# A gated recurrence followed by a gated unit: from per-batch units of six windows to a planned stream of flattened 512-token blocks

**Chip and metric.** One core of one Trainium2 chip runs the whole program. The time is device microseconds (us). A run is several executions, of which the median is quoted; single executions of the changed kernel spread by about 1.4%, those of the kernel before by 0.6%. The program does not leave its one core. The engines are called PE (matrix multiply; PEld is its weight load), DVE (VectorE, elementwise work and scans), ACT (ScalarE, tanh, exp and square root), POOL (GpSimd) and SP (issues transfers). SBUF is the on-chip memory, and PSUM is the memory that takes PE's products.

## The reference, cut to what matters

```python
# B, S, D = 4, 6336, 256; float32 in and out
a_t     = exp(8 * sigmoid(r_gate) * log(clip(sigmoid(a_param))))     # per token and channel
x_gated = sqrt(max(1 - a_t*a_t, 1e-6)) * sigmoid(i_gate) * x
for t in range(S):                                                   # recurrence over time
    h = a_t[:, t] * h + x_gated[:, t]
    y[:, t] = h
gate = sigmoid(causal 5-tap convolution of y over time, per channel)
val  = y @ w_val
out  = (gate * val) @ w_out
```

The recurrence is the only thing that orders the tokens, and it starts anew at each of the four batches. The kernel writes every sigmoid as 0.5 + 0.5 tanh, so that ACT's tanh and exp follow each other without loading another activation table. The square root does not: in the trace of the kernel before, a table load stands in front of each of the 12 square-root instructions and another behind each.

## The kernel before

Channels lie on the 128 partitions (two halves, h) and time on the free axis. A batch of 6336 tokens is cut into twelve windows of 512 and one of 192; six windows make a unit (6, 6 and 1 for each batch). A unit runs tanh and exp for all its windows, then one square root over the whole unit, then the scans. The output half (`backend`) of a window runs two windows later.

```python
unit_list = [win_list[i0:i0 + 6] for i0 in range(0, len(win_list), 6)]
...
for b in range(B):
    for unit in unit_list:
        for (wt0, wnt) in unit:
            # loads in the order x, r, i
            ...
            nc.scalar.activation(out=tri[:], in_=ri[:], func=ACT.Tanh, scale=0.5)
            nc.vector.scalar_tensor_tensor(out=u2[:], in0=ti, scalar=1.0, in1=xt[:], ...)   # "u"
            ...                                        # PE transposes, ACT exp -> ach
            nc.gpsimd.tensor_tensor(out=e_pl[...], in0=ach[...], in1=ach[...], op=ALU.mult) # squares
        nc.scalar.activation(out=n_pl[:, :, 0:utok], in_=e_pl[:, :, 0:utok], func=ACT.Sqrt, ...)
        for wi, (wt0, wnt) in enumerate(unit):
            ...                                        # PE transposes u -> uT
            nc.vector.tensor_tensor(out=xg[...], in0=uT[...], in1=n_pl[...], op=ALU.mult)
            nc.gpsimd.tensor_copy(out=yb[:, :, 0:4], in_=prev_y[:, :, prev_nt:prev_nt + 4])
            for h in range(H):
                nc.vector.tensor_tensor_scan(out=yb[:, h, 4:4 + wnt], data0=ach[:, h, 0:wnt],
                                             data1=xg[:, h, 0:wnt], initial=yb[:, h, 3:4], ...)
            if len(pending) >= 2:
                flush_one()                            # backend of an earlier window
            pending.append((b, wt0, wnt, yb))

def backend(...):
    ...                                                # PE conv -> gp, ACT tanh -> tg, PE -> val
    nc.vector.scalar_tensor_tensor(out=gv[...], in0=tg[...], scalar=1.0, in1=val[...], ...)
    for each pair of 128-token tiles:                  # two in a full window
        ...                                            # PE: ops = gv @ wo
        nc.vector.tensor_scalar(out=osb[:, ii:ii + 2, :], in0=ops[:], scalar1=0.5, ...)
```

The order of the instructions on each engine is left to the framework's scheduler. All output copies are on VectorE.

Of the kernel before, what the change touches and what calls it, by code (L numbers as in the profile page):

```python
# [8 lines left out]
P = 128  # L10
WIN = 512
SUB = WIN // P
UNIT_WIN = 6
CONV_K = 5
C_SCALE = 8.0
FP32 = mybir.dt.float32
BF16 = mybir.dt.bfloat16
ACT = mybir.ActivationFunctionType
ALU = mybir.AluOpType


@with_exitstack
def kernel(
# [14 lines left out]
    H = D // P  # L38

    const = ctx.enter_context(tc.tile_pool(name="const", bufs=1))  # L40

    ident_f = const.tile([P, P], FP32, name="ident_f")
    make_identity(nc, ident_f[:])
    ident_b = const.tile([P, P], BF16, name="ident_b")
    nc.vector.tensor_copy(out=ident_b[:], in_=ident_f[:])

    with tc.tile_pool(name="ps_setup", bufs=2, space=bass.MemoryType.PSUM) as ps_setup:
        ap2 = const.tile([H, P], FP32, name="ap2")
        nc.sync.dma_start(ap2[:], a_param.rearrange("(h p) -> h p", p=P))
        kps = ps_setup.tile([P, H], FP32, name="kps")  # L50
        nc.tensor.transpose(out=kps[:], in_=ap2[0:H, :], identity=ident_f[0:H, 0:H])
        kt = const.tile([P, H], FP32, name="kt")
        nc.scalar.activation(out=kt[:], in_=kps[:], func=ACT.Tanh, scale=0.5)
        ksig = const.tile([P, H], FP32, name="ksig")
        nc.vector.tensor_scalar(out=ksig[:], in0=kt[:], scalar1=0.5, scalar2=0.5,
                                op0=ALU.mult, op1=ALU.add)
        nc.vector.tensor_scalar(out=ksig[:], in0=ksig[:], scalar1=1e-6, scalar2=1.0 - 1e-6,
                                op0=ALU.max, op1=ALU.min)
        kln = const.tile([P, H], FP32, name="kln")
        nc.scalar.activation(out=kln[:], in_=ksig[:], func=ACT.Ln)  # L60
        kf = const.tile([P, H], FP32, name="kf")
        nc.vector.tensor_scalar(out=kf[:], in0=kln[:], scalar1=C_SCALE, scalar2=None, op0=ALU.mult)
        khf = const.tile([P, H], FP32, name="khf")
        nc.vector.tensor_scalar(out=khf[:], in0=kln[:], scalar1=0.5 * C_SCALE, scalar2=None, op0=ALU.mult)

        wrow = const.tile([CONV_K, D], FP32, name="wrow")
        nc.sync.dma_start(wrow[:], moe_conv_w[:, :])
        wcol = []
        for h in range(H):
            wc_ps = ps_setup.tile([P, CONV_K], FP32, name="wc_ps")  # L70
            nc.tensor.transpose(out=wc_ps[:], in_=wrow[0:CONV_K, h * P:(h + 1) * P],
                                identity=ident_f[0:CONV_K, 0:CONV_K])
            wc = const.tile([P, CONV_K], FP32, name=f"wc{h}")
            nc.vector.tensor_copy(out=wc[:], in_=wc_ps[:])
            wcol.append(wc)
        diag = [[None] * CONV_K for _ in range(H)]
        for h in range(H):
            for kk in range(CONV_K):
                dg = const.tile([P, P], BF16, name=f"diag{h}_{kk}")
                nc.vector.tensor_scalar(out=dg[:], in0=ident_f[:], scalar1=wcol[h][:, kk:kk + 1],  # L80
                                        scalar2=None, op0=ALU.mult)
                diag[h][kk] = dg

    b025 = const.tile([P, 1], FP32, name="b025")
    nc.vector.memset(b025[:], 0.25)

    wv = const.tile([P, H, D], BF16, name="wv")
    nc.gpsimd.dma_start(wv[:], moe_w_val.rearrange("(hk p) n -> p hk n", p=P))
    wo = const.tile([P, H, D], BF16, name="wo")
    nc.gpsimd.dma_start(wo[:], moe_w_out.rearrange("(hk p) n -> p hk n", p=P))  # L90


    yring = ctx.enter_context(tc.tile_pool(name="yring", bufs=5))
    aring = ctx.enter_context(tc.tile_pool(name="aring", bufs=8))
    plane = ctx.enter_context(tc.tile_pool(name="plane", bufs=2))
    inp = ctx.enter_context(tc.tile_pool(name="inp", bufs=3))
    u2pool = ctx.enter_context(tc.tile_pool(name="u2pool", bufs=8))
    work = ctx.enter_context(tc.tile_pool(name="work", bufs=3))
    ps_cm = ctx.enter_context(tc.tile_pool(name="ps_cm", bufs=1, space=bass.MemoryType.PSUM))
    ps_conv = ctx.enter_context(tc.tile_pool(name="ps_conv", bufs=1, space=bass.MemoryType.PSUM))  # L100
    ps_val = ctx.enter_context(tc.tile_pool(name="ps_val", bufs=1, space=bass.MemoryType.PSUM))
    ps_out = ctx.enter_context(tc.tile_pool(name="ps_out", bufs=1, space=bass.MemoryType.PSUM))
    win_list = []
    t0 = 0
    while t0 < S:
        nt = min(WIN, S - t0)
        win_list.append((t0, nt))
        t0 += nt
    unit_list = []
    for i0 in range(0, len(win_list), UNIT_WIN):  # L110
        unit_list.append(win_list[i0:i0 + UNIT_WIN])
    max_unit_tok = UNIT_WIN * WIN

    def subtiles(nt):
        res = []
        p0 = 0
        j = 0
        while p0 < nt:
            npj = min(P, nt - p0)
            res.append((j, p0, npj))  # L120
            p0 += npj
            j += 1
        return res

    pending = []
    pstores = []

    def flush_store():
        if pstores:
            dst, srcap = pstores.pop(0)  # L130
            nc.sync.dma_start(dst, srcap)

    def backend(wb, wt0, wnt, yb):
        gp = ps_conv.tile([P, H, WIN], FP32, name="gp", tag="gp")
        for h in range(H):
            for kk in range(CONV_K):
                nc.tensor.matmul(  # L137
                    out=gp[:, h, 0:wnt],
                    lhsT=diag[h][kk][:],
                    rhs=yb[:, h, kk: kk + wnt],  # L140
                    start=(kk == 0), stop=(kk == CONV_K - 1),
                )
        tg = work.tile([P, H, WIN], BF16, name="tg", tag="tg")
        nc.scalar.activation(out=tg[:, :, 0:wnt], in_=gp[:, :, 0:wnt], func=ACT.Tanh, scale=0.5)  # L144
        val = ps_val.tile([P, H, WIN], FP32, name="val", tag="val")
        for m in range(H):
            for hk in range(H):
                nc.tensor.matmul(  # L148
                    out=val[:, m, 0:wnt],
                    lhsT=wv[:, hk, m * P:(m + 1) * P],  # L150
                    rhs=yb[:, hk, 4:4 + wnt],
                    start=(hk == 0), stop=(hk == H - 1),
                )
        gv = work.tile([P, H, WIN], BF16, name="gv", tag="gv")
        nc.vector.scalar_tensor_tensor(  # L155
            out=gv[:, :, 0:wnt], in0=tg[:, :, 0:wnt], scalar=1.0, in1=val[:, :, 0:wnt],
            op0=ALU.add, op1=ALU.mult,
        )
        sts = subtiles(wnt)
        osb = work.tile([P, SUB, D], FP32, name="osb", tag="osb", bufs=4)  # L160
        ii = 0
        full_window = (wnt == WIN)
        while ii < len(sts):
            pair = sts[ii:ii + 2]
            full_pair = len(pair) == 2 and pair[0][2] == P and pair[1][2] == P
            if full_pair:
                ops = ps_out.tile([P, 2, D], FP32, name="ops", tag="ops")
                for (js, p0, npj), slot in zip(pair, (0, 1)):
                    for hk in range(H):
                        nc.tensor.matmul(  # L170
                            out=ops[:, slot, :],
                            lhsT=gv[:, hk, p0:p0 + P],
                            rhs=wo[:, hk, :],
                            start=(hk == 0), stop=(hk == H - 1),
                        )
                nc.vector.tensor_scalar(out=osb[:, ii:ii + 2, :], in0=ops[:], scalar1=0.5, scalar2=None, op0=ALU.mult)  # L176
                if not full_window:
                    p0a = pair[0][1]
                    pstores.append((out[wb, wt0 + p0a:wt0 + p0a + 2 * P, :].rearrange("(j p) d -> p j d", p=P), osb[:, ii:ii + 2, :]))
                ii += 2  # L180
            else:
                (js, p0, npj) = pair[0]
                ops = ps_out.tile([P, 2, D], FP32, name="ops", tag="ops")
                for hk in range(H):
                    nc.tensor.matmul(
                        out=ops[0:npj, 0, :],
                        lhsT=gv[:, hk, p0:p0 + npj],
                        rhs=wo[:, hk, :],
# [138 lines left out]
```

## Time and profile before

| | kernel before |
|---|---|
| time, median of 3 executions (lowest to highest) | 441.89 us (441.31 to 443.02) |
| span of the profiled execution | 440.1 us |
| VectorE (DVE) busy, idle | 363.9, 76.2 us |
| ScalarE (ACT) busy | 291.5 us |
| DVE idle: first 60 us, 60 to 420, the rest | 33.3, 35.6, 7.3 us |

This is DVE's timeline of the kernel before (start, length, engine and line, operation, count, idle before):

```profile
45.70 0.69 DVE L273 TENSOR_TENSOR xg<-uT,n_pl 128x1024 bf16<-128x1024 bf16 x1 [5.50 <-ACT n_pl L257]
46.49 2.46 DVE L281 TENSOR_TENSOR_SCAN yb<-ach,yb,xg 128x512 bf16<-128x512 f32 x2
```

The gated input xg waits 5.5 us for the square root of all six windows, and only then, at 46.5 us, does the recurrence start.

### The profile page before, as it was taken

The page shows a single profiled execution, that of the slowest core. Times are in us where ns is not written, and L with a number is a line of the kernel's source. Part 1 is how long each engine was busy: PE and PEld are TensorE (multiplying, and loading weights), DVE is VectorE, ACT ScalarE, POOL GpSimd, SP SyncE. Part 2 cuts the span into 40 slices and gives each one's busy share as a digit, 9 for nine tenths or more (in the row PEclk, how much of TensorE's full clock was granted, in tenths as well). Part 3 has the DMA queues.
Part 4 walks back from the last instruction along what each step waited for, and adds up shares of the span by engine and source line. Part 5 has one row for each costly group of instructions (what it writes and reads, how often), then busy time and mean ns, then how long its engine had stood idle before and what let it go on. Part 6 is the DMA issues. An engine that isn't in the chain of part 4 may idle for free.

```text
span 440.1 us, 5342 instructions
## 1 busy us (share of the span) xinstructions
PE 293.1 (67%) x1931; PEld 168.7 (38%) x1931; DVE 363.9 (83%) x386; ACT 291.5 (66%) x253; POOL 120.3 (27%) x112
## 2 busy tenths in 40 slices
PE   0221777658884595969684689558876485758994
PEld 0221344334453253535343245233543243424442
DVE  2242899769997799879999899969997599978984
ACT  0988836792969847696958746897465984593111
POOL 2252202700535216402542202802063143300000
PEclk9999999889989598769999599988998689958998
DMA  8999958788769975896978887999886962211233
GB/s 236 348 348 348 316 182 252 257 257 254 238 214 314 331 222 177 273 337 209 295 234 251 275 277 241 283 297 316 251 266 206 335 207 95 73 70 49 95 125 133
DMA packets 105544, 104.43 MB, mean 237 GB/s; under 512 B 3623, under 2 KB 105518, under 8 KB 105518
## 3 DMA queue, kind: packets, MB, share of 16 engines
q1 hardware_dynamic: 104974, 103.83, 74.4%
q0 software_dynamic: 544, 0.26, 0.4%
q8 instruction: 15, 0.25, 0.2%
q14 instruction: 11, 0.09, 0.1%
HBM read 78.39 MB, written 25.95 MB: 237 GB/s over the span
## 4 chain that ended last, share of the span: by engine, by line
DVE 48%; ACT 20%; issue 13%; PE 11%; DMA 5%; POOL 2%; SPq 1%; DVEq 0%; POOLq 0%; ACTq 0%
DVE yb L281 24%; ACT n_pl L257 10%; DVE gv L155 8%; DVE osb L176 8%; DVE xg L273 6%; DMA ri<-in_i_gate_dram 5%; PE ops L170 3%; ACT tri L233 3%; ACT ach L252 3%; PE gp L137 3%; DVE u L234 2%; PE val L148 2%; POOL e_pl L255 2%; ACT L257 2%; PE srT L245 1%
## 5 line engine op out<-in xcount | busy, mean ns | idle before, releaser
L137 PE MATMUL gp<-yb,diag 128*128 128x512 bf16 (+1 forms) x520 | 139.2, 402 | 13.6 <-ACT tg L144 12.1
L281 DVE TENSOR_TENSOR_SCAN yb<-ach,yb,xg 128x512 bf16<-128x512 f32 (+1 forms) x104 | 144.9, 1431 | 1.2
L255 POOL TENSOR_TENSOR e_pl<-ach 128x1024 f32<-128x1024 f32 (+1 forms) x52 | 107.4, 2077 | 74.3 <-ACT ach L252 74.2
L144 ACT ACTIVATE tg<-gp 128x1024 bf16<-128x1024 f32 (+1 forms) x52 | 51.1, 983 | 88.4 <-PE gp L137 84.3
L170 PE MATMUL ops<-wo,gv 128*128 128x256 bf16 x384 | 62.9, 290 | 59.8 <-DVE gv L155 41.7
L233 ACT ACTIVATE tri<-ri 128x2048 bf16<-128x2048 f32 x48 | 90.4, 1910 | 1.9 <-DMA ri<-in_i_gate_dram 1.8
L252 ACT ACTIVATE ach<-srT,khf 128x512 f32<-128x512 bf16 (+1 forms) x104 | 71.9, 757 | 29.0 <-PE srT L245 28.8
L234 DVE SCALAR_TENSOR_TENSOR u<-tri,xt 128x1024 bf16<-128x1024 bf16 x48 | 69.0, 1437 | 25.2 <-ACT tri L233 25.2
L176 DVE TENSOR_SCALAR osb<-ops 128x512 f32<-128x512 f32 x96 | 65.0, 677 | 16.4 <-PE ops L170 16.1
L279 POOL COPY yb<-yb 128x8 bf16<-128x8 bf16 x48 | 10.8, 225 | 226.9 <-DVE yb L281 178.4
L137 PEld LDWEIGHTS <-diag 128*128 128x128 bf16 x520 | 50.4, 103 | 58.0 <-ACT tg L144 10.2
L170 PEld LDWEIGHTS <-gv 128*128 128x128 bf16 x384 | 36.3, 102 | 92.6 <-DVE gv L155 61.3
L267 PE MATMUL uT<-ident_b,u 128*128 128x128 bf16 (+1 forms) x400 | 40.5, 248 | 35.0 <-DVE xg L273 34.7
L155 DVE SCALAR_TENSOR_TENSOR gv<-tg,val 128x1024 bf16<-128x1024 bf16 (+1 forms) x52 | 60.0, 1154 | 3.1 <-ACT tg L144 3.1
L148 PE MATMUL val<-yb,wv 128*128 128x512 bf16 (+1 forms) x208 | 56.6, 388 | 0.0
L245 PE MATMUL srT<-ident_b,tri 128*128 128x128 bf16 (+1 forms) x400 | 36.2, 237 | 28.5 <-ACT tri L233 18.3
L273 DVE TENSOR_TENSOR xg<-uT,n_pl 128x1024 bf16<-128x1024 bf16 (+1 forms) x52 | 33.9, 653 | 23.1 <-ACT n_pl L257 22.7
L267 PEld LDWEIGHTS <-u 128*128 128x128 bf16 (+1 forms) x400 | 33.2, 112 | 50.5 <-issue 42.8
L257 ACT ACTIVATE n_pl<-e_pl,b 128x6144 bf16<-128x6144 f32 (+1 forms) x12 | 45.8, 3815 | 3.8 <-POOL e_pl L255 3.6
L245 PEld LDWEIGHTS <-tri 128*128 128x128 bf16 (+1 forms) x400 | 29.0, 106 | 39.6 <-ACT tri L233 20.3
L148 PEld LDWEIGHTS <-wv 128*128 128x128 bf16 x208 | 20.9, 102 | 16.8 <-issue 2.8
L257 ACT ACT_TABLE_LOAD x12 | 15.4, 1283 | 0.2
(32 smaller groups left out, 45.2 us busy)
## 6 DMA issues: line engine op xcount, KB each, us to landing
xt<-in_x_dram SPq DMA_DIRECT2D x48, 512.0 KB, 5.0
ri<-in_r_gate_dram SPq DMA_DIRECT2D x48, 512.0 KB, 5.8
ri<-in_i_gate_dram SPq DMA_DIRECT2D x48, 512.0 KB, 6.2
out_dram<-osb SPq DMA_DIRECT2D x48, 512.0 KB, 3.5
xt<-in_x_dram SPq DMA_DIRECT2D x4, 128.0 KB, 3.4
ri<-in_r_gate_dram SPq DMA_DIRECT2D x4, 128.0 KB, 3.3
ri<-in_i_gate_dram SPq DMA_DIRECT2D x4, 128.0 KB, 3.3
out_dram<-osb SPq DMA_DIRECT2D x4, 128.0 KB, 1.8
```

Source lines behind the costliest of these rows:

```text
L137: nc.tensor.matmul(out=gp[:, h, 0:wnt], lhsT=diag[h][kk][:], rhs=yb[:, h, kk: kk + wnt], start=(kk == 0), stop=(kk == CONV_K - 1),)
L148: nc.tensor.matmul(out=val[:, m, 0:wnt], lhsT=wv[:, hk, m * P:(m + 1) * P], rhs=yb[:, hk, 4:4 + wnt], start=(hk == 0), stop=(hk == H - 1),)
L155: nc.vector.scalar_tensor_tensor(out=gv[:, :, 0:wnt], in0=tg[:, :, 0:wnt], scalar=1.0, in1=val[:, :, 0:wnt], op0=ALU.add, op1=ALU.mult,)
L170: nc.tensor.matmul(out=ops[:, slot, :], lhsT=gv[:, hk, p0:p0 + P], rhs=wo[:, hk, :], start=(hk == 0), stop=(hk == H - 1),)
L176: nc.vector.tensor_scalar(out=osb[:, ii:ii + 2, :], in0=ops[:], scalar1=0.5, scalar2=None, op0=ALU.mult)
L233: nc.scalar.activation(out=tri[:], in_=ri[:], func=ACT.Tanh, scale=0.5)
L234: nc.vector.scalar_tensor_tensor(out=u2[:], in0=ti, scalar=1.0, in1=xt[:], op0=ALU.add, op1=ALU.mult)
L252: nc.scalar.activation(out=ach[:, h, 0:wnt], in_=srT[:, h, 0:wnt], func=ACT.Exp, scale=khf[:, h:h + 1], bias=khf[:, h:h + 1])
L255: nc.gpsimd.tensor_tensor(out=e_pl[:, :, wc0:wc0 + wnt], in0=ach[:, :, 0:wnt], in1=ach[:, :, 0:wnt], op=ALU.mult)
L257: nc.scalar.activation(out=n_pl[:, :, 0:utok], in_=e_pl[:, :, 0:utok], func=ACT.Sqrt, scale=-0.25, bias=b025[:, 0:1])
L267: nc.tensor.transpose(out=uT[:, h, p0:p0 + npj], in_=u2[0:npj, j, h * P:(h + 1) * P], identity=ident_b[0:npj, 0:npj],)
L281: nc.vector.tensor_tensor_scan(out=yb[:, h, 4:4 + wnt], data0=ach[:, h, 0:wnt], data1=xg[:, h, 0:wnt], initial=yb[:, h, 3:4], op0=ALU.mult ...
```

## The change

Its intent is to keep DVE and ACT both occupied by one stream that does not stop at batch ends. It has six parts.

1. The batches are flattened to 25344 tokens: 49 windows of 512 and one of 256. Windows that straddle a batch end are scanned in two segments, so the four short windows vanish.
2. Planes and pools become rings of eleven slots (a, e, u) and seven (y); the square root writes in place. The other pools change a little too: two product buffers for xg, gv and tg instead of three, three output buffers instead of four, and a scan takes its first value straight from the previous window and not from POOL's copy of it.
3. The square-root batches grow from one window (1, 3, 3, 4, 4, 5 and so on, as the plan finds work) instead of six at once.
4. The output copies go to DVE or ACT, whichever the plan says can start sooner (53 and 46), and the 0.5 moves into the weights.
5. The inputs are issued r, i, x, so that tanh can begin before x is there; three input buffers instead of four.
6. A list schedule built from a table of costs decides the order of all instructions, and the framework is told to keep it.

```diff
+NS = 11
+NY = 7
+NIN = 3
+MIN_UNIT = [1, 2, 3, 4]
+COST = dict(load=4.5, tanh=1.9, u2=1.3, ..., scan=2.7, ..., osbD=0.64, osbA=0.62, sq=0.88, table=1.3, ...)
+def make_plan(frac):
... each step: of all operations whose inputs are done, take the one that can start first
+            for e, eng in (("D", "DVE"), ("A", "ACT")):
+                cand("osb", eng, COST["osb" + e], [("out", q), ("store", qwin[q][0] - NOSB)], 0.5, q)
...
+            low = (nsq - at("scan")) * (COST["xg"] + COST["scan"]) <= 2 * COST["table"] + COST["sq"] * n
+            enough = n >= min(MIN_UNIT[min(len(units), len(MIN_UNIT) - 1)], nw - nsq)
+            if stuck or (low and enough):
+                cand("sq", "ACT", ...)
...
-    for b in range(B):
-        for unit in unit_list:
+    with tc.manual_schedule():
...
+        aring = rings.tile([P, NS, H, WIN], FP32, name="aring")
+        ering = rings.tile([P, NS, H, WIN], FP32, name="ering")
+        uring = rings.tile([P, NS, SUB, D], BF16, name="uring")
+        yring = rings.tile([P, NY, H, YW], BF16, name="yring")
...
-                        initial=yb[:, h, 3:4],
+                        initial=0.0 if fresh else py[:, h, pend - 1:pend],
...
-                nc.vector.tensor_scalar(out=osb[:, ii:ii + 2, :], in0=ops[:], scalar1=0.5, ...)
+            if eng == "DVE":
+                nc.vector.tensor_copy(out=dst, in_=ops[:])
+            else:
+                nc.scalar.copy(out=dst, in_=ops[:])
...
+        for (t, op, i, eng, n) in plan:
+            ops_by_name[op](i, eng, n)
```

## The prediction

> **What bounds the kernel now.** I read five views in this order: busy time by engine, busy time by stretch, the vector engine's waits, groups by shape, and the timeline around one square-root batch. All are of the kernel before.
>
> ```profile
> PE 293.1 (67%) x1931; PEld 168.7 (38%) x1931; DVE 363.9 (83%) x386; ACT 291.5 (66%) x253; POOL 120.3 (27%) x112
> HBM read 78.39 MB, written 25.95 MB: 237 GB/s over the span
> ```
>
> VectorE (DVE) is the fullest engine, yet it idles 440.1 - 363.9 = 76.2 us. The bytes are not the limit: a 1/40 slice of the early load-only phase moves 348 GB/s, and 104.4 MB at that rate are 300 us.
>
> ```profile
> 0.00:60.00 60.00, 19.85 (x124) 12.34 (x125) 26.68 (x38) 41.38 (x33) 16.05 (x19) 1.00 1.00 313
> 60.00:420.00 360.00, 260.20 (x1729) 149.03 (x1727) 324.44 (x331) 246.65 (x217) 104.02 (x92) 0.89 0.73 231
> 420.00:440.10 20.10, 13.08 (x82) 7.35 (x80) 12.80 (x19) 3.46 (x4) 0.19 (x1) 0.91 0.33 115
> ```
>
> Columns: stretch, length, busy us of PE, weight loads, DVE, ACT, POOL, then clock, DMA share, GB/s. DVE idles 33.3 us in the first 60, 35.6 (10%) in the middle and 7.3 at the end.
>
> ```profile
> DVE u L234 <- ACT tri L233: 25.2, 8, 7.9
> DVE xg L273 <- ACT n_pl L257: 22.7, 8, 5.5
> DVE osb L176 <- PE ops L170: 16.1, 22, 1.4
> ```
>
> The waits say why: for the first tanh results, for the square-root batch (one batch of six windows must be complete before any scan of it; the first scan starts at 46.5 us), and for the output product held in one PSUM buffer.
>
> ```profile
> L281 DVE TENSOR_TENSOR_SCAN yb<-ach,yb,xg 128x512 bf16<-128x512 f32 x96 | 135.2, 1446 | 1.1
> L234 DVE SCALAR_TENSOR_TENSOR u<-tri,xt 128x1024 bf16<-128x1024 bf16 x48 | 69.0, 1437 | 25.2 <-ACT tri L233 25.2
> L176 DVE TENSOR_SCALAR osb<-ops 128x512 f32<-128x512 f32 x96 | 65.0, 677 | 16.4 <-PE ops L170 16.1
> L155 DVE SCALAR_TENSOR_TENSOR gv<-tg,val 128x1024 bf16<-128x1024 bf16 x48 | 57.8, 1205 | 3.1 <-ACT tg L144 3.1
> L273 DVE TENSOR_TENSOR xg<-uT,n_pl 128x1024 bf16<-128x1024 bf16 x48 | 32.5, 678 | 23.1 <-ACT n_pl L257 22.7 <-PE uT L267 0.4
> ...
> L257 ACT ACT_TABLE_LOAD x12 | 15.4, 1283 | 0.2
> ```
>
> **What the Trainium skill says, and whether the trace agrees.** "ScalarE: Activation LUTs", section "What ACT_TABLE_LOAD costs": tables are loaded by set, exp and sqrt lie in different ones, and a switch is given as 1283 ns of load plus about 1380 of drain. The load agrees (1283); the drain does not appear:
>
> ```profile
> 86.63 5.42 ACT L257 ACTIVATE n_pl<-e_pl,b 128x6144 bf16<-128x6144 f32 x1 [0.75 <-POOL e_pl L255]
> 92.06 1.28 ACT L144 ACT_TABLE_LOAD   x1
> 93.35 1.02 ACT L144 ACTIVATE tg<-gp 128x1024 bf16<-128x1024 f32 x1
> ```
>
> The load starts 0.01 us after the square root ends and the tanh follows it at once, so I charge 1.28 us a switch. The same section gives an ACTIVATE with immediate operands as 186 ns + 0.833 ns an element: about 0.61 us for a 512-wide output copy on ACT (an estimate; no such copy runs before). "SBUF — State Buffer", section "Who interferes with whom": a DVE instruction with two SBUF inputs contends with a GpSimd instruction reading SBUF. The trace agrees: the scan's median is 1265 ns but its mean 1446, u's 1215 and 1437; both read two SBUF operands beside the squaring on POOL. The excess is 96 x 0.18 + 48 x 0.22 = 28 us. "VectorE: DVE Perf Modes", section "The perf-mode tier table": an fp32 operand in PSUM allows no faster mode. Hence folding 0.5 into the output weights makes the DVE copy no cheaper than today's 677 ns.
>
> **The change part by part.** The built order gives the counts: 49 windows of 512 tokens and one of 256 (49.5 in place of 48 full and 4 of 192), 53 output copies on DVE and 46 on ACT, 12 square-root units of 1, 3, 3, 4, 4, 5, 4, 4, 5, 5, 6 and a last 5.5 windows, in 23 instructions instead of 12.
>
> DVE work. One window without copies: (135.2 + 69.0 + 57.8 + 32.5) / 48 = 6.14 us; times 49.5 is 304. Copies: 53 x 0.677 = 36. Setup: 3. Sum 343 in row sums. The rows of before sum to 384 against 363.9 busy, since neighbours overlap, so I scale by 0.948: **325 us**, 39 less. Of that about 29 are the copies moved and about 10 are the short windows of 192, which cost nearly a full scan (1255 ns a half) for three eighths of the tokens.
>
> ACT work. tanh 49.5 x 1.91 = 95; exp 99 x 0.72 = 71; gate tanh 49.5 x 1.02 = 50; square root: a six-window call takes 5.42, so with the page's 0.28 us fixed part about 0.86 a window: 49.5 x 0.86 + 23 x 0.28 = 49; tables 27 x 1.28 = 35, as many as now; copies 46 x 0.61 = 28. Sum 328, and row sums against busy are 299 to 291.5 before: **319 us**, 28 more. So ACT and DVE come out almost equal. PE keeps its work (minus about 2% for padding) and POOL its 50 squarings; both have room.
>
> Start. Inputs are now issued r, i, x, so the first tanh needs 1 MB rather than 1.5 MB: about 8 us rather than 11.25. From there: tanh 1.9, transposes 1.0, exp 1.45, square 1.9, a second tanh in front of the load, table 1.28, square root 1.1, product 0.7: first scan near 18 us instead of 46.5. But unit two (windows 1 to 3) needs a table back, three tanh, three exp pairs, a gate tanh and a table, about 15 us of ACT, so its scans begin near 35. By then DVE has done about 15 us of work (setup 3, five u 6, one scan pair, product, gate, copies). After that it has as much work as ACT's next unit lasts (near 15 us each). **Start idle about 20 us, from 33.**
>
> End. The last unit leaves about eight windows of scans; the last window is half-sized. After its last scan come conv, gate, product, copy and store: about 8 us, of which DVE works 2 to 3. **End idle about 5 us.**
>
> DVE's path: 325 + 20 + 5 = 350. ACT's path: all but its last 9 gate tanh and 11 copies (319 - 16 = 303) must be done before the last scans can start, plus about 5 idle at the start, plus some 38 of DVE work and drain behind the last square root: 346. Two bounds within 1%.
>
> Middle. Two engines each at over 90%, fed in a fixed order, stall one another whenever a duration differs from the plan: a squaring that stretches a scan, a late load (three input buffers instead of four). DVE loses 10% there now; the batches come when the scans are about to run out instead of behind six windows, and the copies take the sooner engine, so I halve it: 5% of 340, **17 us**. This is the softest number. 350 + 17 = 367 of span, and 1.8 more for the measured time (441.9 against 440.1): **369 us**, 16% less.
>
> **The rivals.** First, ACT becomes the bound. For: 319 against 325, plus 12 batches whose table loads stop gate tanh and exp alike. Against: it waits 84 us for conv results today, waits that the interleaving can fill. If it also idles 8%, the time is near 380. Second, contention on the shared port grows: DVE leaves fewer gaps, so more of the 50 squarings fall beside a scan or u. If each costs 1 us rather than 28 / 48 = 0.6, that is 20 us more: 385 to 390. Third, loads become the bound: 104 MB in 365 us is 286 GB/s, 82% of the 348 seen, with three buffers. For: a store waiting in the in-order queue holds the loads behind it. Against: beyond the start, tanh waited 1.8 us for loads before, and a buffer has about three windows (20 us) to be refilled, while a load lands in 5 to 6 us. At worst 10 us. Fourth, the plan holds nearly perfectly and the middle loses 2%: 356.
>
> **Range and chances.** The rivals make 356 to 390; contention and ACT stalls together are possible but partly overlap in time. I take 355 to 386. To be within 2% it would have to lose 64 us of the 73 expected, more than any rival costs: faster 0.96, same 0.03, slower 0.01.
>
> **What would show it.** DVE busy 320 to 330 and ACT 315 to 325; first scan at 17 to 20 us; DVE idle near 20 us by 50 us; DVE waits for the square root well under 22.7 us beyond the start; table load still 1283 with no drain; DVE copies still near 677 ns and ACT copies near 610. A scan mean above 1500 ns means the contention rival; tanh waiting over 10 us for loads beyond the start means the load rival; ACT busier than DVE in the middle with DVE waiting for tanh or square root means the ACT rival. I am wrong if DVE busy does not fall by about 39 us, or if the middle loses over 10%.

## The result

| | before | after |
|---|---|---|
| time, median of 4 executions (lowest to highest) | 442.45 us (441.31 to 443.86) | 376.86 us (374.66 to 379.99) |
| span of the profiled execution | 440.1 us | 372.5 us |
| DVE busy, idle | 363.9, 76.2 us | 334.6, 37.9 us |
| ACT busy | 291.5 us | 312.4 us |

The ratio is 0.8516 (95% interval 0.8469 to 0.8563): 15% faster, and the outputs are correct. Ratios are the mean time of one kernel's fast executions over that of the other's in the same rounds, so not quite the ratio of the medians quoted here.

Busy time by engine (us, share of the span, instructions) and the bytes, after the change:

```profile
PE 272.4 (73%) x1933; PEld 159.9 (43%) x1933; DVE 334.6 (90%) x326; ACT 312.4 (84%) x298; POOL 138.3 (37%) x111
HBM read 78.39 MB, written 25.95 MB: 280 GB/s over the span
```

The span fell by 67.6 us. DVE's busy time gives 363.9 - 334.6 = 29.3 of it, DVE's idle time 76.2 - 37.9 = 38.3. So more than half of the gain is waiting that went, not work that moved.

Busy time by stretch after the change, with the columns that the prediction names:

```profile
0.00:60.00 60.00, 29.72 (x201) 17.75 (x202) 38.54 (x50) 51.40 (x46) 20.84 (x21) 0.89 1.00 313
60.00:360.00 300.00, 235.44 (x1686) 137.62 (x1685) 291.78 (x273) 257.03 (x248) 117.50 (x90) 0.95 0.86 279
360.00:372.50 12.50, 7.27 (x50) 4.50 (x47) 4.24 (x5) 3.96 (x6) 0.00 (x0) 0.93 0.41 147
```

DVE idles 21.5 us in the first 60, 300 - 291.78 = 8.2 us in the middle and 8.3 at the end. The middle, which lost 10% before, loses 2.7%.

DVE's waits after the change (us in total, times, longest):

```profile
DVE osb L367 <- PE ops L356: 8.0, 10, 1.7
DVE uring L246 <- ACT tri L240: 6.9, 6, 3.2
DVE xg L290 <- ACT ering L277: 6.2, 2, 5.0
```

These answer the three waits that the prediction shows, 16.1, 25.2 and 22.7 us before. The one for the square root happens twice in the whole program, both times at the start.

Groups by shape after the change (busy us, mean ns, then the idle time before and what ended it):

```profile
L306 DVE TENSOR_TENSOR_SCAN yring<-aring,yring,xg 128x512 bf16<-128x512 f32 x90 | 134.5, 1535 | 0.6
L246 DVE SCALAR_TENSOR_TENSOR uring<-tri,xt 128x1024 bf16<-128x1024 bf16 x49 | 66.8, 1369 | 7.0 <-ACT tri L240 6.9
L367 DVE COPY osb<-ops 128x512 f32<-128x512 f32 x53 | 36.1, 682 | 9.2 <-PE ops L356 8.0
...
L369 ACT COPY osb<-ops 128x512 f32<-128x512 f32 x46 | 27.2, 592 | 22.2 <-PE ops L356 19.1 <-issue 2.4 <-ACT tri L240 0.5
L277 ACT ACT_TABLE_LOAD x12 | 15.4, 1283 | 0.2
```

The copy costs DVE 682 ns, as the multiplying one cost 677, and ACT 592. The scan's mean rose from 1446 to 1535 ns, the only operation on DVE that became clearly dearer; u's mean fell from 1437 to 1369. The table load is as it was. On POOL the copy of the last four columns of a window became nearly three times as dear, before and after:

```profile
L279 POOL COPY yb<-yb 128x8 bf16<-128x8 bf16 x48 | 10.8, 225 | 226.9 <-DVE yb L281 178.4 <-PE srT L245 18.4 <-PE gp L137 11.9
L304 POOL COPY yring<-yring 128x8 bf16<-128x8 bf16 x49 | 31.6, 644 | 77.4 <-DVE yring L306 77.4
```

Little waits for it (PE's convolution, 1.3 us in all), and no run isolates why.

DVE's timeline around the first two square-root batches:

```profile
17.72 0.69 DVE L290 TENSOR_TENSOR xg<-uT,ering 128x1024 bf16<-128x1024 bf16 x1 [1.23 <-ACT ering L277]
18.45 2.34 DVE L306 TENSOR_TENSOR_SCAN yring<-aring,xg 128x512 bf16<-128x512 f32 x2
...
36.21 0.69 DVE L290 TENSOR_TENSOR xg<-uT,ering 128x1024 bf16<-128x1024 bf16 x1 [5.01 <-ACT ering L277]
36.94 2.46 DVE L306 TENSOR_TENSOR_SCAN yring<-aring,yring,xg 128x512 bf16<-128x512 f32 x2
```

The recurrence begins at 18.5 us instead of 46.5, does one window, and goes on at 36.9 when the next three windows have their square root.

### The profile page after: what moved, and what is told of

Read it like the earlier page. It is cut to its first block, busy times and chain, and to the rows that moved or that the text cites. A ratio compares the mean times of both kernels' runs of the same rounds, so it can differ in the third digit from the quotient of the medians.

```text
span 372.5 us, 5299 instructions
## 1 busy us (share of the span) xinstructions
PE 272.4 (73%) x1933; PEld 159.9 (43%) x1933; DVE 334.6 (90%) x326; ACT 312.4 (84%) x298; POOL 138.3 (37%) x111
## 4 chain that ended last, share of the span: by engine, by line
DVE 34%; ACT 23%; issue 19%; PE 14%; DMA 5%; POOL 2%; DVEq 0%; ACTq 0%
DVE yring L306 13%; DVE uring L246 8%; DVE gv L344 7%; ACT tri L240 6%; ACT ering L277 5%; PE gp L321 5%; PE ops L356 4%; ACT aring L257 4%; DMA xt<-in_x_dram 3%; DVE xg L290 3%; PE val L338 3%; ACT tg L327 3%; DVE osb L367 2%; ACT L327 2%; ACT L277 2%
## 5 line engine op out<-in xcount | busy, mean ns | idle before, releaser
L262 POOL TENSOR_TENSOR ering<-aring 128x1024 f32<-128x1024 f32 (+1 forms) x50 | 105.7, 2121 | 140.9 <-ACT aring L257 121.8
L321 PE MATMUL gp<-yring,diag 128*128 128x512 bf16 (+4 forms) x530 | 124.5, 384 | 24.7 <-DVE yring L306 14.2
L306 DVE TENSOR_TENSOR_SCAN yring<-aring,yring,xg 128x512 bf16<-128x512 f32 (+4 forms) x98 | 139.5, 1464 | 0.7
L240 ACT ACTIVATE tri<-ri 128x2048 bf16<-128x2048 f32 (+1 forms) x50 | 94.4, 1907 | 0.0
L321 PEld LDWEIGHTS <-diag 128*128 128x128 bf16 x530 | 50.8, 102 | 83.5 <-issue 16.3
L257 ACT ACTIVATE aring<-srT,khf 128x512 f32<-128x512 bf16 (+1 forms) x100 | 71.8, 791 | 3.4 <-PE srT L228 2.2
L246 DVE SCALAR_TENSOR_TENSOR uring<-tri,xt 128x1024 bf16<-128x1024 bf16 (+1 forms) x50 | 67.4, 1356 | 7.0 <-ACT tri L240 6.9
L344 DVE SCALAR_TENSOR_TENSOR gv<-tg,val 128x1024 bf16<-128x1024 bf16 (+1 forms) x50 | 59.7, 1194 | 2.5 <-PE val L338 1.7
L338 PE MATMUL val<-yring,wv 128*128 128x512 bf16 (+4 forms) x212 | 52.1, 371 | 5.3 <-DVE gv L344 5.3
L277 ACT ACTIVATE ering<-ering,b 128x3072 bf16<-128x3072 f32 (+2 forms) x21 | 47.0, 2280 | 0.1
L369 ACT COPY osb<-ops 128x512 f32<-128x512 f32 x46 | 27.2, 592 | 22.2 <-PE ops L356 19.1
L367 DVE COPY osb<-ops 128x512 f32<-128x512 f32 x53 | 36.1, 682 | 9.2 <-PE ops L356 8.0
L228 PE MATMUL uT<-ident_b,uring 128*128 128x128 bf16 x396 | 33.3, 232 | 15.0 <-DVE xg L290 14.7
L290 DVE TENSOR_TENSOR xg<-uT,ering 128x1024 bf16<-128x1024 bf16 (+1 forms) x50 | 33.7, 675 | 6.2 <-ACT ering L277 6.2
```

What stands on the lines that cost most here:

```text
L228: nc.tensor.transpose(out=dst[:, h, j * P:(j + 1) * P], in_=src[:, j, h * P:(h + 1) * P], identity=ident_b[:])
L240: nc.scalar.activation(out=tri[:, :, 0:nj, :], in_=ri[:, :, 0:nj, :], func=ACT.Tanh, scale=0.5)
L246: nc.vector.scalar_tensor_tensor(out=uring[:, g % NS, 0:nj, :], in0=tri[:, 1, 0:nj, :], scalar=1.0, in1=xt[:, 0:nj, :], op0=ALU.add, op1=A ...
L257: nc.scalar.activation(out=aring[:, g % NS, h, 0:ntok[g]], in_=srT[:, h, 0:ntok[g]], func=ACT.Exp, scale=khf[:, h:h + 1], bias=khf[:, h:h ...
L262: nc.gpsimd.tensor_tensor(out=ering[:, g % NS, :, 0:ntok[g]], in0=a, in1=a, op=ALU.mult)
L277: nc.scalar.activation(out=nring[:, sl:sl + k, 0:H * WIN], in_=ering[:, sl:sl + k].rearrange("p s h t -> p s (h t)"), func=ACT.Sqrt, scale ...
```

## Experiments

Twelve runs, in three calls, each with its own runs of the kernel before on the same chip. The changed kernel itself came to ratio 0.8516 beside its own runs of before and to 0.8463 in the last call, so ratios of different calls are compared with about 0.6% of doubt. Differences in us are taken from 376.86, the first call's figure, unless another is named; only the last call has its own run of the changed kernel. All medians are of four executions.

### The copies alone on DVE, same order

```diff
-            if eng == "DVE":
+            if True:
```

> The changed kernel in the same issue order, but all 99 output copies on DVE (46 moved back from ACT). Theory, DVE sets the pace (in the changed kernel it is busy 291.8 of the 300 us from 60 to 360): DVE busy rises by 46 x 0.61 = 28 us to about 362, ACT falls by 27 to about 285, and nearly all of it shows: about 403 us. Rival, ACT and DVE share the pace and ACT gains what DVE loses: half of it, about 390 us.

Measured: 407.13 us (405.91 to 408.83), ratio 0.9197 (0.9163 to 0.9232). Busy time by engine:

```profile
PE 284.3 (70%) x1933; PEld 162.2 (40%) x1933; DVE 362.6 (89%) x372; ACT 289.8 (71%) x252; POOL 133.4 (33%) x111
```

DVE is 362.6 - 334.6 = 28.0 us busier, and the time is 407.13 - 376.86 = 30.3 us longer. From 60 to 340 us DVE is busy 267.25 of 280 us (95%):

```profile
60.00:340.00 280.00, 206.00 (x1428) 118.31 (x1426) 267.25 (x260) 219.59 (x190) 107.47 (x79) 0.91 0.88 283
```

So with this order DVE sets the time, and what is put on it appears nearly in full: sharing the copies is worth 30 us here.

### The copies alone on ACT, same order

```diff
-            if eng == "DVE":
+            if False:
```

> The changed kernel in the same issue order, but all 99 output copies on ACT (53 moved from DVE at 0.59 us each). Theory, the split is near its balance: ACT busy rises by 31 us to about 343 and sets the pace, DVE falls to about 302: about 390 us, so the split beats both ends. Rival, DVE alone is short and ACT has room (43 idle us of the 300 in the middle): about 365 us.

Measured: 393.07 us (389.40 to 394.37), ratio 0.8873 (0.8817 to 0.8930). DVE is busy 302.6 us, ACT 337.7. From 60 to 340 us ACT has 259.8 of 280 us and DVE only 233.0; DVE waits for tanh 21.5 us, for the value product 18.7 and for the gate tanh 16.8:

```profile
60.00:340.00 280.00, 208.67 (x1476) 123.75 (x1499) 233.01 (x196) 259.80 (x272) 121.09 (x82) 0.92 0.89 287
DVE uring L246 <- ACT tri L240: 21.5, 16, 3.2
```

ACT is the fuller engine now, and the time is 16 us worse although DVE lost 32 us of work. The two runs together show that, in this order, neither engine alone should have the copies. The order was planned for the split; a plan made for all copies on one engine was not run.

### The framework's order in place of the planned one

```diff
-    with tc.manual_schedule():
+    if True:
```

The program is the same, copies, batches and rings too; only the order on the engines is left to the framework.

> The changed kernel with the same operations and buffers, but its order left to the framework's own scheduler instead of the list schedule's (correct result). Theory, the explicit order is what keeps the middle full: DVE idle between 60 and 360 us rises from 8 (2.7%) to about the 10% of the kernel before, +22 us, about 398 us. Rival, buffers, shared copies and small first batches carry the gain and any sensible order does: within 6 us, about 380 us.

Measured: 401.38 us (399.82 to 405.63), ratio 0.9080 (0.9019 to 0.9141). Its middle stretch, and its largest DVE wait:

```profile
60.00:360.00 300.00, 220.83 (x1554) 131.46 (x1555) 269.67 (x254) 258.23 (x244) 104.31 (x87) 0.89 0.84 271
```

```profile
DVE osb L367 <- PE ops L356: 25.2, 25, 3.0
```

DVE is busy 331.5 us in all, no more than with the planned order; but in the middle it idles 300 - 269.67 = 30.3 us instead of 8.2. So the order alone is worth 401.38 - 376.86 = 24.5 us, and it is won in idle time: 25 copies wait on DVE for an output product that PE has not finished, with everything behind them. The framework's order also changes tables more often, 33 loads instead of 27, and ACT is 8 us busier.

### Six windows in each square-root batch at least

```diff
-MIN_UNIT = [1, 2, 3, 4]
+MIN_UNIT = [6]
```

> The changed kernel planned with square-root batches of at least six windows from the first on (8 batches instead of 12). Theory, the growing batches are worth what they save at the start: first scan near 46 us instead of 18.4, DVE idle in the first 60 us near 35 instead of 21.5, middle unchanged, about 391 us. Rival, the eight table loads saved on ACT (4 batches, 10 us) and fuller batches give it back: within 4 us of the changed kernel, about 379 us.

Measured: 380.76 us (379.62 to 381.34), ratio 0.8592 (0.8561 to 0.8623); eight batches of 5 to 8 windows. First 60 us, and the first scan:

```profile
0.00:60.00 60.00, 20.86 (x153) 13.62 (x154) 27.14 (x39) 48.09 (x42) 22.31 (x20) 1.00 1.04 319
```

```profile
42.50 2.34 DVE L306 TENSOR_TENSOR_SCAN yring<-aring,xg 128x512 bf16<-128x512 f32 x2
```

The first scan is 24 us later, and DVE idles 54.2 us in all instead of 37.9. That is 16.3 us more, 11.4 of it in the first 60 us, where the theory held about 13.5. But the time is only 4 us longer, near the rival's number, because DVE is busy 325.1 us, 9.5 less. The plan answered the late start by giving six more copies to ACT (47 on DVE instead of 53; 6 x 0.68 = 4 us), and the scan's mean fell to 1467 ns. A late start was partly made good by moving work away from the engine that was late. Growing batches are worth some 4 us by this call and 6 against the last call's 374.94; the interval of the ratio just overlaps that of the first run of the changed kernel (0.8469 to 0.8563) and lies clear of the last one's (0.8426 to 0.8500). Either is far less than the 24 us by which the first scan comes earlier.

### No wide read of SBUF by POOL

```diff
-            nc.gpsimd.tensor_tensor(out=ering[:, g % NS, :, 0:ntok[g]], in0=a, in1=a, op=ALU.mult)
+            nc.gpsimd.memset(ering[:, g % NS, :, 0:ntok[g]], 0.25)
+            nc.gpsimd.tensor_tensor(out=ering[:, g % NS, :, 0:1], in0=a[:, :, 0:1], in1=a[:, :, 0:1], op=ALU.mult)
```

The result is wrong: a constant takes the place of the square, and one column keeps the dependence.

> Wrong result on purpose. The squaring on POOL reads only one column per half and fills the rest with a constant, so POOL hardly reads SBUF; waits, order and all else stay. Theory, the excess of the scan's mean over its median (1535 against 1270 ns) and of u's (1369 against 1210) is contention with POOL's reads: means fall to about 1270 and 1220, DVE busy falls by about 32 us to about 302, ACT (312 busy) then sets the pace: about 358 us. Rival, the excess is something else (semaphores, PSUM): means stay above 1450 and 1330 and the time within 4 us of 377.

Measured: 359.26 us (358.46 to 360.52), ratio 0.8116 (0.8089 to 0.8143). Groups by shape (busy us, mean ns):

```profile
L307 DVE TENSOR_TENSOR_SCAN yring<-aring,yring,xg 128x512 bf16<-128x512 f32 x90 | 110.5, 1269 | 0.6
...
L246 DVE SCALAR_TENSOR_TENSOR uring<-tri,xt 128x1024 bf16<-128x1024 bf16 x49 | 59.2, 1214 | 8.8 <-ACT tri L240 8.7
```

The scan's mean is 1269 ns instead of 1535 and u's 1214 instead of 1369. DVE's busy time falls by 334.6 - 301.8 = 32.8 us, that is 32.8 / 50 = 0.66 us for each squaring. POOL still writes the whole plane here (46.6 us of memset). So the extra time in the scan and u comes from POOL's reading, and not from the operands or the rings. The time falls by only 17.6 us: ACT, at 310.9 us busy, does not get shorter, and DVE now idles 55 us.

### A plan that believes the scan is dearer, or a little dearer

```diff
-COST = dict(..., scan=2.7, ...)
+COST = dict(..., scan=3.4, ...)      # first run; 3.0 in the second
```

The table has 2.7 us for a window's scans, and the trace shows about 2 x 1.5. Does a plan with a truer figure do better?

> The changed kernel planned with a scan cost of 3.4 instead of 2.7, one constant (the pair measured 2.9 to 3.1 with the contention). The plan then puts 37 copies on DVE and 62 on ACT and makes 10 batches. Theory, the plan took DVE for faster than it is: 16 copies fewer are 10 us less of DVE, middle as full: about 367 us. Rival, the plan is then off elsewhere and ACT, at about 320 busy, holds the scans up: 377 us or more.

Measured with 3.4: 381.31 us (380.34 to 383.38), ratio 0.8627 (0.8583 to 0.8671). The plan leaves 37 copies on DVE and puts 62 on ACT; DVE's work falls by 13 us to 321.4, but its idle time rises by 19 to 57, with waits for tanh (14.2 us) and for the output product (13.4). Slower, by 1.2%, although DVE (321.4) and ACT (315.5) are now nearly equally busy. The plan also makes 10 batches instead of 12, so this is not the split alone.

> The changed kernel planned with a scan cost of 3.0 instead of 2.7 (45 copies on DVE, 54 on ACT, 11 batches). Theory, the plan with the cost nearest to the measured scan pair (2.9 to 3.1) waits least and moves 5 us off DVE: about 371 us. Rival, as with 3.4, whatever leaves DVE comes back as waits: between 376 and 382 us.

Measured with 3.0: 373.81 us (373.44 to 374.79), ratio 0.8439 (0.8398 to 0.8481), 45 copies on DVE. The unaltered kernel of the same call has 374.94 and an interval that overlaps: no difference is shown. Plans with 45 and with 53 copies on DVE take the same time here; they also differ in their batches (11 and 12).

### The kernel before with half of the copies on ACT

```diff
+                if ii == 0:
                     nc.vector.tensor_scalar(out=osb[:, ii:ii + 2, :], in0=ops[:], scalar1=0.5, ...)
+                else:
+                    nc.scalar.mul(osb[:, ii:ii + 2, :], ops[:], 0.5)
```

> The kernel before with one of the two output copies of each window on ACT, nothing else. Theory, the copies are worth their DVE time only where DVE is kept full: in the kernel before DVE idles 10% in the middle in waits for batches and products, so of the 31 us taken from DVE about 10 to 15 show: about 430 us. Rival, DVE time is the whole matter: about 412 us.

Measured: 448.00 us (447.50 to 448.15), ratio 1.0125 (1.0081 to 1.0169): a little slower, clear of the noise though under 2%. Theory and rival both failed. Busy time by engine, and DVE's and ACT's waits:

```profile
PE 300.8 (67%) x1896; PEld 173.1 (39%) x1931; DVE 315.2 (71%) x338; ACT 315.9 (71%) x301; POOL 112.2 (25%) x112
```

```profile
DVE u L237 <- ACT tri L236: 49.3, 20, 7.8
DVE xg L276 <- ACT n_pl L260: 34.4, 8, 5.5
DVE gv L155 <- ACT tg L144: 14.8, 7, 2.4
```

```profile
ACT osb L179 <- PE ops L170: 34.9, 24, 3.1
```

DVE lost 48.7 us of work, and won nothing: its idle time went from 76.2 to 131.1 us. Only 65.0 - 32.8 = 32.2 us of the work are the copies; most of the rest is that scans and u were stretched less (means of 1332 and 1291 ns instead of 1446 and 1437). The copies stand in ACT's queue and wait there 34.9 us for PE's product; DVE's waits for ACT grow, tanh 25.2 to 49.3 us, square root 22.7 to 34.4, gate tanh 3.1 to 14.8. How much of that comes from the copies' waits and how much from their 28.6 us of work on ACT was not separated, and the framework was free to reorder. What is shown is that in this kernel waits set the pace and not DVE's work: the work went and the waits grew.

### The kernel before with growing first units

```diff
-        for unit in unit_list:
+        for unit in (unit_list if b else [win_list[0:1], win_list[1:4], win_list[4:8], win_list[8:13]]):
```

> The kernel before with square-root units of 1, 3, 4 and 5 windows in the first batch element instead of 6, 6 and 1; the rest as before. Theory, the early first scan is worth the start idle it saves: first scan near 21 us instead of 46.5, DVE idle in the first 60 us near 22 instead of 33, about 431 us. Rival, the time saved at the start is lost again in the following stalls: within 4 us of 442.

Measured: 436.75 us (436.11 to 437.33), ratio 0.9874 (0.9837 to 0.9911). The first scan begins at 24.3 us, and DVE's start idle is 25.1 us instead of 33.3; the time falls by 442.70 - 436.75 = 6 us, about half of what the theory held. This is about the same few us that the batch sizes are worth in the changed kernel.

### The changed kernel again, and two variants that could beat it

> The changed kernel unaltered, as the yardstick for the other runs of this call. Expected 377 us; if it differs from that by more than 4 us, small differences between calls say nothing.

Measured: 374.94 us (374.13 to 375.95), ratio 0.8463 (0.8426 to 0.8500); span 372.1, DVE busy 334.2. The trace agrees with that of the first run.

```diff
-            nc.gpsimd.tensor_tensor(out=ering[...], in0=a, in1=a, op=ALU.mult)
+            if g % 3 == 1:
+                nc.scalar.activation(out=ering[...], in_=a, func=ACT.Square)
+            else:
+                nc.gpsimd.tensor_tensor(out=ering[...], in0=a, in1=a, op=ALU.mult)
```

> The changed kernel with every third window's squaring on ACT instead of POOL (17 of 50, about 1.04 us each), same order. Theory, POOL's reads beside DVE cost DVE about 33 us over 50 squarings and ACT has about 43 idle us in the middle: DVE busy falls by about 11 us, ACT rises by 17 to about 329, about 368 us. Rival, ACT is too nearly full for the fixed order: what DVE gains comes back as waits for tanh and gate tanh, 377 us or more.

Measured: 371.90 us (369.56 to 372.75), ratio 0.8385 (0.8342 to 0.8428). A third of the squares on ACT takes 17.5 us of busy time from DVE (316.7) and adds 14 to ACT (326.7). The gain is 3 us, at the edge of what the intervals tell apart: ACT is now the fuller engine, and DVE's waits for tanh (12.8 us) and for the output product (17.5) are longer than in the first run (6.9 and 8.0). DVE won 17.5 us for 17 squarings, 1.03 each, where about 11 were expected from the average of 0.66: the cost of one squaring is not constant. The scan shows most of it:

```profile
L309 DVE TENSOR_TENSOR_SCAN yring<-aring,yring,xg 128x512 bf16<-128x512 f32 x90 | 125.2, 1432 | 0.7
```

```diff
-MIN_UNIT = [1, 2, 3, 4]
+MIN_UNIT = [1, 1, 2, 2, 3, 4]
```

> The changed kernel planned with smallest batches of 1, 1, 2, 2, 3, 4 windows; the plan then makes 15 batches instead of 12 and puts 51 copies on DVE. Theory, the start is limited by how soon a batch's windows are in: second batch's scan near 27 us instead of 36.9, start idle about 5 us less, about 372 us. Rival, the three more batches are 6 more table loads (8 us of ACT) just where ACT is full, and the start gains nothing: 377 us or more.

Measured: 370.18 us (369.71 to 371.64), ratio 0.8360 (0.8323 to 0.8397). DVE's timeline, first and second batch:

```profile
18.90 2.34 DVE L306 TENSOR_TENSOR_SCAN yring<-aring,xg 128x512 bf16<-128x512 f32 x2
...
27.72 2.46 DVE L306 TENSOR_TENSOR_SCAN yring<-aring,yring,xg 128x512 bf16<-128x512 f32 x2
```

The second scan comes at 27.7 us instead of 36.9, and the start idle falls from 21.5 to 60 - 40.92 = 19.1 us. It is 1.3% faster than the changed kernel of the same call, with intervals apart, and correct: the fastest correct kernel here. It has three more batches than the changed kernel, and ACT is 9.6 us busier than in its neighbour (322.2 against 312.6), which costs nothing that shows. The two profiled executions differ by 2.2 us only, all of it at the start; the 4.8 us between the medians are more than the trace explains.

### What stays open

- Flattening was not run alone, and its share (the prediction says 10 us of DVE work) is argued.
- That the shared copies need the planned order is not shown. The kernel before differs from the changed one in all six parts, and the framework's order was not run with the copies on DVE alone.
- The rings, the third input buffer and the order r, i, x were not run apart either.
- The squares on ACT and the finer start were not combined.
- The values need not add up: order 24.5, shared copies 30 and batches 4 to 6 are each the loss when that one is taken out of the finished kernel.

## Why the prediction was right, and where its steps were off

The prediction said 369.0 us, between 355 and 386. The measured 376.86 is 7.9 above this figure, inside the range and in the direction given 0.96. Of these, 5.5 us are in the span (372.5 against 367); the rest is mostly that the profiled execution, at 374.66 us, was the fastest of the four.

| term of the sum | predicted | measured | off by |
|---|---|---|---|
| DVE busy | 325 | 334.6 | +9.6 |
| start idle | 20 | 21.5 | +1.5 |
| middle idle | 17 | 8.2 | -8.8 |
| end idle | 5 | 8.3 | +3.3 |
| span | 367 | 372.5 | +5.5 |

**DVE busy** was mis-sized in the term "One window without copies". It carried the scan and u over from before with their contention unchanged. The scans' rows measured 149.4 us against 135.2 / 48 x 49.5 = 139.4, and u's 67.4 against 71.2; copies (36.1), gate product (59.7) and xg (33.7) came as stated. The rows sum to 350 against 343, and overlap is a little less than the 0.948 assumed. The run without POOL's reads has 122.0 us in the scans' rows, so the whole excess is POOL's reading: 27 us in the scans now, where 96 x 0.18 = 17 were seen before. In u it is less than before, about 7.5 us for 10.6. Together that is about 35 us where 28 were carried over. So the second rival, "contention on the shared port grows", came in a small part: some 6 of its 20 us, and 0.66 us for each squaring against the 0.6 of before and the 1 us that it named. The scan's mean passed its mark of 1500 ns, while u's fell.

The prediction named a fall of about 39 us in DVE's busy time as a condition: "I am wrong if" it does not come. It fell by 29.3. By that sign this step was wrong, although the total held.

One reading in this term was also wrong. "Cost nearly a full scan (1255 ns a half)" is a mean of two kinds: of the four pairs of 192-wide scans, two took 1.11 and 1.13 us and two 3.74. The shortest half took 0.59 us; the rest is most likely the same contention, but no run isolates it.

**The middle** was called the softest number, and it was: halving 10% to 5% was a guess, and 2.7% came. The fourth rival's figure of 2% for a plan that holds was nearer. The run in the framework's order shows what the guess missed: the same work loses 30.3 us there, so the idle time depends on the order much more than on how full the two engines are. These two misses, +9.6 and -8.8, nearly cancel by luck, so the total looks better than its terms.

**Start:** right in its times: first scan "near 18 us" (18.45), second unit "near 35" (36.94). **End:** 8.3 instead of 5; DVE's last instruction ends at 366.96 us, and 5.5 us of product, copies on ACT and store follow, with small waits ahead of it.

**ACT:** 312.4 against 319, below its mark of 315. Its rows came as computed (near 328), and only overlap more than assumed: 27 table loads at 1283 ns, copies 592 ns against the estimated 610, square roots of one, two and three windows 1136, 1989 and 2854 ns, which fit the estimate of 0.28 us and 0.86 a window. (That exp and sqrt lie in different sets, which the prediction puts in the section on the load's cost, stands in the next section of that page, "Table sets: the hidden batching unit".) That ACT and DVE bound the kernel nearly equally was right: taking 33 us of work from DVE brings 17.6, and moving all copies either way costs 16 or 30 us. **Loads:** the third rival does not show; no tanh waits for a load beyond the start, at 280 GB/s.

**The gain's cause:** the part text names the copies (29 us) and the windows (10 us) as DVE's saving and treats the order as a matter of idle time: 39 from busy, and 76.2 - 42 = 34 from idle. It came as 29.3 and 38.3. The copies' rows did fall by 65.0 - 36.1 = 29 us, and the contention took back a part. What the prediction did not say is that moving the copies need not pay at all. In the kernel before it did not: 48.7 us of DVE work less and 1.25% slower.

## What to carry to other kernels

Ask first whether the fullest engine is short of time or waits. Here taking 28 us of copies from it brought 30 us where it idled 3% of the middle, and nothing where it idled 10%. So look at the order before moving work. A moved instruction also waits on its new engine (34.9 us for the copies on ACT in the kernel before); place it where its input is already done. Small batches at the start are cheap to have and worth 4 to 6 us. A cost table for a list schedule need not be exact: 2.7 and 3.0 us for a scan pair gave the same time, and 3.4 one that is 1.2% longer. Equal busy times are no goal in themselves: the plan with 3.4 had them.

## What the Trainium skill lacked or had wrong

- "ScalarE: Activation LUTs", section "What ACT_TABLE_LOAD costs", adds a drain of about 1380 ns to each switch. No run here shows it: the 27 loads of either kernel take 1283 ns each, and wherever the next activation waits for nothing else it begins 0.01 us after the load ends. A switch costs 1.28 us, so small square-root batches are about half as dear as the page suggests.
- "SBUF — State Buffer", section "Who interferes with whom", says that a DVE instruction with two SBUF inputs contends with GpSimd's reads but gives no size for this mix. Here one 128x1024 squaring on POOL, of about 2.1 us, costs DVE 0.66 us of busy time on average (32.8 us over 50), and the 17 that were moved to ACT in another run 1.03 us each: the scan's mean is 1535 ns with the squarings and 1269 without, u's 1369 and 1214. How much of that reaches the time depends on the second-fullest engine, 17.6 us here.
